# Recurrent attention with an MLP behind it: decay sums over the product of two tokens' w, the diagonal term added on VectorE, and unit 5 transposed by DMA as well

## The chip, the cores and the metric

The kernel runs on one core of one Trainium2 chip. The metric is the device time of one execution in microseconds (us), as the median of several executions. The profile's span, from the first to the last instruction of one profiled execution, is 1.7 to 1.9 us shorter than the device time of the same execution. Stage lengths are read from profiles.

Short names: PE is TensorE (the matrix engine), DVE is VectorE, ACT is ScalarE, POOL is GpSimd.

## The reference

A linear attention with a decay per channel runs over 768 tokens, for 4 sequences and 8 heads of 48 channels. Its output goes through an MLP of 384 by 2048 by 384 with a Gelu.

```python
def _attn_ref(r, k, v, w, u):                       # each (4, 8, 768, 48); u (8, 48)
    state = zeros((B, H, D, D))
    for t in range(S):
        ...                                         # rt, kt, vt, wt: r, k, v, w of token t
        cur = einsum('bhd,bhe->bhde', u[None] * kt, vt)
        y[:, :, t] = einsum('bhd,bhde->bhe', rt, state + cur)
        state = wt[:, :, :, None] * state + einsum('bhd,bhe->bhde', kt, vt)
    return y

def _moe_ref(x, w_in, w_out):                       # x (3072, 384)
    h = x @ w_in                                    # (3072, 2048)
    g = 0.5 * h * (1.0 + tanh(c * (h + 0.044715 * h**3)))
    return g @ w_out
```

The kernel works in *units*: 256 tokens of one sequence, 12 units in all, numbered 0 to 11. Two neighbouring tokens share a partition (the index `t2` tells them apart). The recurrence within a chunk is turned into matrix products: the factors of the decay come from sums of log w over earlier tokens, which are products with a triangular matrix of ones.

## The kernel before

The kernel gives eight PSUM banks to three pools. Two hold MLP tiles (`h`), two hold the down projection (`o`), and four serve everything of the attention (`a`).

```python
ps_h = tile_pool(name="ps_h", bufs=2, space=PSUM)
ps_o = tile_pool(name="ps_o", bufs=2, space=PSUM)
ps_a = tile_pool(name="ps_a", bufs=4, space=PSUM)
```

The decay sums take log w of both tokens of a pair, and add the two on PE by accumulating two matmuls for each sum. The exponentials go back into PSUM, except unit 5's (`sbuf=True`), which are copied to SBUF so that its sums leave their banks early.

```python
def ln(q):
    lw = logws[q % 3]                       # [128, 2, 8, 64]
    ACT.activation(out=lw[:, :, :, 0:D].rearrange("p t h d -> p h t d"),
                   in_=ld["w", q].rearrange("p h (t d) -> p h t d", t=2), func=AF.Ln)

def a1(q, pool=None, tag="a"):
    lw = logws[q % 3]
    x, z = ((pool or ps_a).tile([P, 512], FP, ...) for i in range(2))
    for dst, tri in ((x, strict), (z, incl)):
        for t2 in range(2):
            PE.matmul(dst[:, 0:HD], tri, lw[:, t2, :, 0:D], start=(t2 == 0), stop=(t2 == 1))
    for g in range(G):
        for t2 in range(2):
            PE.matmul(z[:, ds(HD + 2 * g, 2)], lw[:, t2, ds(2 * g, 2), :], ones2, ...)

def exps(q, sbuf=False): ...                # ACT: e1 = exp(-z), fq = exp(x), al = exp(ends)

def prep(q):                                # four DVE products: kk (two, with e1), rq (two, with fq)
    for dst, t2, x, dec in ((kk, 0, kw, e1), (kk, 1, kt[:, :, D:2*D], e1),
                            (rq, 0, rt[:, :, 0:D], fq), (rq, 1, rw, fq)):
        DVE.tensor_tensor(out=dst[...], in0=gjd(x), in1=dec..., op=AL.mult)
    ...                                     # am on POOL
```

The attention of a unit is a generator whose steps are woven between the MLP groups of the unit before it. `...` marks cuts.

```python
PE_T = (6, 6)                               # units below 6 are transposed on PE, later ones by DMA

def attention(q):
    if q < PE_T[...]: a2(q, 0), a2(q, 1); yield     # transposes of kk, rq
    a3(q, 0); yield                         # scores, round 0: 16 matmuls, then two DVE mask products
    a3(q, 1); yield                         # scores, round 1
    a4(q); a4p(q); yield                    # y: scores times v, plus diagonal term; p: state products
    a5(q, 0); yield                         # y += rq times state, first half; then ACT copies y to xs
    a5(q, 1); yield
    a6(q); yield                            # transpose xs for the MLP

def a4(q):
    ...                                     # 32 matmuls y <- scores, v
    for t2 in range(2):                     # the diagonal term, by selection matmuls
        for c2 in range(2):
            PE.matmul(ys[c2][:, :, :], sel...[rows, t2, :], st["vsc", q][rows, t2, :, :], ...)

def a5(q, c2):
    ...
    ACT.activation(out=st["xs", q][:, c2, :], in_=ys[c2]..., func=AF.Copy)

def mm1(q, i):                              # one MLP group: 6 matmuls into one ps_h bank, then its Gelu
    h = ps_h.tile([P, 2, WIN], FP, tag="h")
    ...
    ACT.activation(out=st["g", q][:, ds(2*i, 2), :], in_=h, func=AF.Gelu_apprx_tanh)

for q in range(3, NU):
    att = attention(q + 1) if q + 1 < NU else iter(())
    for i in range(8):
        mm1(q, i)
        if i >= 4:
            mm2(q, 0, (2*i - 8, 2*i - 7))   # two down-projection matmuls
        if i in ((0, 1, 2, 4, 5, 6, 7) if q + 1 < max(PE_T) else (1, 2, 4, 5, 6)):
            next(att, None)
        if q == 3 and i == 4:
            prep(5); ...
        ...                                 # prep_w, prep_a (POOL) at i == 0; a1, prep_b at i == 6
    ...
```

The whole kernel:

## Time and profile before

The time before is 207.69 us, the median of the four runs beside which the changed kernel was timed (207.44 to 208.52). I call *stage q* the stretch from the first MLP matmul of unit q to that of unit q+1. It holds the MLP of unit q and the attention of unit q+1. The stage lengths are read from the timeline of PE:

| stretch | us | what limits it |
|---|---|---|
| up to stage 0 | 22.82 | loads, first unit's attention |
| stages 0, 1, 2, 3 | 19.08, 16.11, 17.88, 16.50 | PE, held in places by DVE |
| stage 4 | 15.40 | PE; still with PE transposes of unit 5 |
| stages 5 to 8 | 14.15, 14.16, 14.15, 14.15 | PE |
| stages 9, 10 | 13.30, 13.30 | PE; no decay sums left to do |
| stage 11 and end | 15.30 | PE, then the last store |

These are two lines of the profile page of the kernel before: busy time and share of the span by engine, and the chain of waits that ended last, by engine.

```profile
PE 184.5 (89%) x2328; PEld 132.9 (64%) x2328; DVE 129.1 (63%) x223; ACT 123.9 (60%) x197; POOL 114.2 (55%) x114
...
PE 75%; DVE 15%; POOL 3%; DMA 2%; ACT 2%; issue 1%; DVEq 0%; ACTq 0%; POOLq 0%
```

Averages over the span hide the stages. This is the busy time by stretch (start and end, length, then the busy time of each engine and its instructions) for stages 3, 7 and 9 of the kernel before (behind the last busy time stand granted clock, DMA share and GB/s):

```profile
75.89:92.39 16.50, 15.20 (x208) 11.32 (x206) 14.06 (x25) 9.82 (x17) 12.21 (x12) 1.00 0.49 111
...
136.10:150.25 14.15, 14.15 (x184) 10.32 (x183) 8.00 (x16) 9.80 (x17) 9.37 (x9) 1.00 0.79 163
...
164.40:177.70 13.30, 13.30 (x171) 9.73 (x170) 5.67 (x11) 8.12 (x12) 0.19 (x1) 1.00 0.39 71
```

In the later stretches PE is busy for the whole stage, so there what leaves PE should leave the time, while DVE (8.00 of 14.15 us) has room. In stage 3 PE is idle for 1.3 us while DVE is busy for 14.06 of 16.50 us. There, work taken from PE may become waiting. The idle time is one wait. In this timeline of PE the columns are start, duration from first start to last end, what, and in brackets the idle time before it and what ended it:

```profile
79.64 0.24 PE L272 MATMUL mt_0_0_1423<-TT_1_1395,TT_0_1384 48*64 48x128 bf16 x2 [1.30 <-DVE TT_1_1395 L255]
```

PE waits for DVE to copy unit 4's transposes out of PSUM before it can start the scores. DVE comes to those copies late because of products ahead of them. One of those, which has both inputs in SBUF, takes 1.84 us (timeline of DVE, before):

```profile
73.37 1.84 DVE L188 TENSOR_TENSOR rw_1332<-r_211,w_201 128x384 f32<-128x384 f32 x1
```

The parts that the change takes from PE have these costs in the PE-bound stages. The duration column of a row reaches past the start of the next row (the two matmuls of `cum_0` last 0.49 us, and the next row starts 0.33 us after their start), so a cost is read from start to start:

```profile
126.96 0.32 PE L301 MATMUL y_0_2376<-vsc_1914,sel 64*128 64x384 bf16 x1
...
127.29 0.20 PE L318 MATMUL p_0_2414<-vb_1724,kk_126 64*128 64x96 bf16 x1
...
130.03 0.49 PE L172 MATMUL cum_0_2469<-logw_122,strict 128*128 128x384 bf16 x2
130.36 0.49 PE L172 MATMUL cum_1_2470<-logw_122,incl 128*128 128x384 bf16 x2
130.68 0.34 PE L176 MATMUL cum_1_2470<-ones_102,logw_122 128*128 128x2 bf16 x8
130.88 0.81 PE L369 MATMUL h_7_2487<-xT_2222,w_in_sb 128*128 128x256 bf16 x6
```

The diagonal term occupies PE from 126.96 to 127.29 (0.33 us) and the decay sums from 130.03 to 130.88 (0.85 us). Last, the MLP groups around the two score rounds of a unit, in the same timeline:

```profile
136.75 0.82 PE L369 MATMUL h_1_2582<-xT_2507,w_in_sb 128*128 128x256 bf16 x6
137.50 0.24 PE L272 MATMUL mt_0_0_2590<-TT_1_2249,TT_0_2246 48*64 48x128 bf16 x2
...
137.85 0.83 PE L369 MATMUL h_2_2611<-xT_2507,w_in_sb 128*128 128x256 bf16 x6
138.61 0.24 PE L272 MATMUL mt_1_0_2619<-TT_1_2249,TT_0_2246 48*64 48x128 bf16 x2
...
138.96 0.83 PE L369 MATMUL h_3_2640<-xT_2507,w_in_sb 128*128 128x256 bf16 x6
139.62 0.82 PE L369 MATMUL h_4_2648<-xT_2507,w_in_sb 128*128 128x256 bf16 x6
140.28 0.49 PE L378 MATMUL o_0_2656<-w_out_sb,g_2564 128*128 128x384 bf16 x2
```

An MLP group alone takes 0.66 us from start to start (138.96 to 139.62). With a score round behind it, it takes 1.10 to 1.11 us (136.75 to 137.85, and 137.85 to 138.96). So the two rounds cost 2.21 − 2 × 0.66 = 0.89 us, and part of that was, by my estimate, the cost of going from one kind of matmul to the other and back.

### The profile page before, as it was taken

To read this page: it belongs to the slowest core of one execution; us is meant where nothing else is said; L and a number is where in the kernel's file an instruction comes from. 1 tells how busy PE (TensorE), PEld (TensorE's weight loads), DVE (VectorE), ACT (ScalarE), POOL (GpSimd) and SP (SyncE) were. 2 spreads that over 40 slices of the span, in tenths; PEclk is the share of its full clock that TensorE was granted. 3 is DMA by queue.
4 is the path that set the end of the run, shared out by engine and by line. 5 is a ranking of instruction groups with operands and counts; after the bars stand their busy time and mean duration, and the time that the engine had idled before them with its cause. 6 is when DMAs were issued, how large, how long until landed. Compare 5 with 4: busy or idle time off the path is not lost.

```text
span 206.3 us, 5543 instructions
## 1 busy us (share of the span) xinstructions
PE 184.5 (89%) x2328; PEld 132.9 (64%) x2328; DVE 129.1 (63%) x223; ACT 123.9 (60%) x197; POOL 114.2 (55%) x114
## 2 busy tenths in 40 slices
PE   0566697998999897999999999999999999999991
PEld 0344484676676565767767767767677677676760
DVE  7846969858667799698665666576373653352111
ACT  3355456765567473594495594785774757457550
POOL 3877737494894988949369468286396300000000
PEclk9999999999999999999999999999999999999998
DMA  6999999999979414906897795985975161200203
GB/s 160 273 392 344 327 340 302 238 264 262 225 189 227 102 41 106 239 22 99 189 220 103 164 246 92 231 180 105 229 92 89 43 102 41 67 12 19 61 0 76
DMA packets 70024, 33.58 MB, mean 163 GB/s; under 512 B 63984, under 2 KB 69232, under 8 KB 70000
## 3 DMA queue, kind: packets, MB, share of 16 engines
q1 hardware_dynamic: 70000, 33.24, 70.1%
q8 instruction: 18, 0.29, 0.6%
q14 instruction: 6, 0.05, 0.1%
HBM read 25.36 MB, written 4.72 MB: 146 GB/s over the span
## 4 chain that ended last, share of the span: by engine, by line
PE 75%; DVE 15%; POOL 3%; DMA 2%; ACT 2%; issue 1%; DVEq 0%; ACTq 0%; POOLq 0%
DMA w_89<-in_w_dram 2%; PE o_1_3620 L378 1%; PE o_0_1489 L378 1%; PE o_0_2921 L378 1%; PE o_0_2373 L378 1%; PE o_0_2088 L378 1%; PE o_0_3574 L378 1%; PE o_0_2656 L378 1%; PE o_0_3396 L378 1%; PE o_1_3512 L378 1%; PE o_1_3292 L378 1%; PE o_1_3072 L378 1%; PE o_1_2808 L378 1%; PE o_1_2537 L378 1%; PE o_1_2252 L378 1%; PE o_1_1967 L378 1%
## 5 line engine op out<-in xcount | busy, mean ns | idle before, releaser
L369 PEld LDWEIGHTS <-w_in_sb 128*128 128x128 bf16 x576 | 54.1, 99 | 13.2 <-issue 3.0
L157 ACT ACT_TABLE_LOAD x13 | 16.7, 1283 | 0.9 <-PEq L585 0.7
L159 ACT ACT_TABLE_LOAD x12 | 15.4, 1283 | 0.2
L172 PEld LDWEIGHTS <-strict 128*128 128x128 bf16 x24 | 1.8, 100 | 6.6 <-issue 4.9
L172 PE MATMUL cum_0_219<-logw_122,strict 128*128 128x384 bf16 x2 | 0.8, 502 | 5.5 <-ACT logw_122 L163 5.5
L386 DVE COPY ob_3616<-o_0_3574 128x384 f32<-128x384 f32 x1 | 0.6, 558 | 7.7 <-PE o_0_3574 L378 7.7
L378 PEld LDWEIGHTS <-g_440 128*128 128x128 bf16 x32 | 2.8, 97 | 3.0 <-issue 1.4
L378 PE MATMUL o_0_558<-w_out_sb,g_440 128*128 128x384 bf16 x16 | 3.6, 327 | 1.1 <-DVE w_out_sb L86 1.1
L378 PEld LDWEIGHTS <-g_3533 128*128 128x128 bf16 x32 | 3.1, 98 | 1.6
L378 PEld LDWEIGHTS <-g_2829 128*128 128x128 bf16 x32 | 3.1, 98 | 1.5
L378 PEld LDWEIGHTS <-g_1689 128*128 128x128 bf16 x32 | 3.1, 98 | 1.5
L378 PEld LDWEIGHTS <-g_1375 128*128 128x128 bf16 x32 | 3.1, 98 | 1.5
L378 PEld LDWEIGHTS <-g_2281 128*128 128x128 bf16 x32 | 3.1, 98 | 1.5
L378 PEld LDWEIGHTS <-g_2564 128*128 128x128 bf16 x32 | 3.1, 98 | 1.5
L378 PEld LDWEIGHTS <-g_3313 128*128 128x128 bf16 x32 | 3.1, 98 | 1.5
L378 PEld LDWEIGHTS <-g_1996 128*128 128x128 bf16 x32 | 3.1, 98 | 1.5
L378 PEld LDWEIGHTS <-g_3093 128*128 128x128 bf16 x32 | 3.1, 98 | 1.5
L207 POOL TENSOR_TENSOR vsc_530<-vb_434,dg_529 128x768 bf16<-128x768 bf16 x1 | 1.7, 1662 | 4.3 <-DVE dg_529 L206 4.3
L378 PEld LDWEIGHTS <-g_745 128*128 128x128 bf16 x32 | 2.8, 98 | 1.7
L172 PEld LDWEIGHTS <-incl 128*128 128x128 bf16 x24 | 2.5, 106 | 2.0 <-issue 0.7
L378 PEld LDWEIGHTS <-g_1046 128*128 128x128 bf16 x32 | 2.7, 97 | 1.6
L242 POOL TENSOR_TENSOR am_708<-blk,al_680 128x384 f32<-128x384 bf16 x2 | 1.9, 987 | 2.9 <-ACT al_680 L222 2.9
(895 smaller groups left out, 645.2 us busy)
## 6 DMA issues: line engine op xcount, KB each, us to landing
wi_157<-in_moe_w_in_dram SPq DMA_DIRECT2D x1, 512.0 KB, 5.0
wi_159<-in_moe_w_in_dram SPq DMA_DIRECT2D x1, 512.0 KB, 6.1
wi_161<-in_moe_w_in_dram SPq DMA_DIRECT2D x1, 512.0 KB, 6.9
wi_163<-in_moe_w_in_dram SPq DMA_DIRECT2D x1, 512.0 KB, 7.7
wi_165<-in_moe_w_in_dram SPq DMA_DIRECT2D x1, 512.0 KB, 8.5
wi_167<-in_moe_w_in_dram SPq DMA_DIRECT2D x1, 512.0 KB, 9.4
w_89<-in_w_dram SPq DMA_DIRECT2D x1, 384.0 KB, 3.7
k_91<-in_k_dram SPq DMA_DIRECT2D x1, 384.0 KB, 4.7
```

Of the source, the lines that this page charges most:

```text
L157: ACT.preload_act_table_set(EXP_SET)
L159: ACT.preload_act_table(AF.Gelu_apprx_tanh)
L172: PE.matmul(dst[:, 0:HD], tri, lw[:, t2, :, 0:D], start=(t2 == 0), stop=(t2 == 1))
L207: POOL.tensor_tensor(out=vsc, in0=vb, in1=dg.rearrange("p h t -> p t h")[:, :, :, None].broadcast_to([P, 2, H, D]), op=AL.mult)
L242: POOL.tensor_tensor(out=am[:, c2], in0=blk.rearrange("p g j d -> p g (j d)"), in1=al[:, :, c2][:, :, None].broadcast_to([P, G, 2 * D]), o ...
L369: PE.matmul(h[:, f, :], w_in_sb[:, cb, ts(ft, P)], xT[:, :, cb, :], start=(f + cb == 0), stop=(cb == NCB - 1), skip_group_check=True)
L378: PE.matmul(st["o", q, c2], g[:, ft, ts(c2, P)], w_out_sb[:, ft, :], start=(ft == 0), stop=(ft == NFT - 1))
L386: DVE.tensor_copy(out=ob[:, c2, :], in_=st.pop(("o", q, c2)))
```

## The change

Four ideas are in it.

1. *Decay sums halved.* log(w0) + log(w1) = log(w0 w1). The product of the two tokens' w is formed first (`ww`, on POOL, for unit 0 on DVE). One Ln of half the elements follows, and the sums need one matmul where they needed two.
2. *Diagonal term on DVE.* From unit 6, the four selection matmuls go, and so do ACT's two copies of y out of PSUM. Four DVE additions bring y out of PSUM and add the diagonal term on the way. They are half-height (64 partitions each), as the two tokens of a pair lie in different halves.
3. *Unit 5 also by DMA transpose.* That takes its 16 transposes off PE and the two copies off DVE. For this its exponentials stay in PSUM (its first sum in an `a` bank, its second in an `o` bank), and its four products move up, ahead of unit 4's state operations.
4. *Score rounds merged* from unit 6: both rounds run behind MLP group 1, instead of behind groups 1 and 2.

The diff, cut to its core:

```diff
-    logws = [pfix.tile([P, 2, H, 64], BF, ...) for i in range(3)]
+    logws = [pfix.tile([P, H, 64], BF, ...) for i in range(3)]
-    PE_T = (6, 6)
+    PE_T = (5, 5)
+    DVE_DIAG = 6
+    MERGE = 6
     def ln(q):
-        ... (both tokens' w)
+        ACT.activation(out=logws[q % 3][:, :, 0:D], in_=st.pop(("ww", q)), func=AF.Ln)
+    def ww(q, eng=POOL):
+        wt = ld["w", q]
+        t = pw2.tile([P, H, D], FP, tag="ww", name=f"ww{q}")
+        eng.tensor_tensor(out=t, in0=wt[:, :, 0:D], in1=wt[:, :, D:2 * D], op=AL.mult)
+        st["ww", q] = t
     def a1(q, ...):
-            for t2 in range(2):
-                PE.matmul(dst[:, 0:HD], tri, lw[:, t2, :, 0:D], start=(t2 == 0), stop=(t2 == 1))
+            PE.matmul(dst[:, 0:HD], tri, lw[:, :, 0:D], start=True, stop=True)
...
     def a4(q):
-        for t2 in range(2):
+        for t2 in range(2 if q < DVE_DIAG else 0):
...
     def a5(q, c2):
+        if q >= DVE_DIAG:
+            for t2 in range(2):
+                rows = ds(64 * t2, 64)
+                DVE.tensor_tensor(out=st["xs", q][rows, c2, :]..., in0=ys[c2][rows, :, :],
+                                  in1=st["vsc", q][ds(64 * c2, 64), t2, :, :], op=AL.add)
+            return
         ACT.activation(out=st["xs", q][:, c2, :], in_=ys[c2]..., func=AF.Copy)
...
     def attention(q):
         a3(q, 0)
-        yield
+        if q < MERGE:
+            yield
         a3(q, 1)
...
         if q == 2:
-            a1(5)
-            exps(5, True)
+            a1(5, (0, 1))
+            exps(5)
...
-            if q == 3 and i == 4:
+            if q == 3 and i == 2:
                 prep(5)
+            if i == 0 and q + 4 < NU:
+                ww(q + 4)
```

More of the change, by code (lines that the diff above doesn't have):

```diff
@@ L125 @@
     make_identity(nc, ident)
-    logws = [pfix.tile([P, 2, H, 64], BF, name=f"logw{i}") for i in range(3)]
+    logws = [pfix.tile([P, H, 64], BF, name=f"logw{i}") for i in range(3)]
     kk_ps = [pfix.tile([P, G, 2, 2, 64], BF, name=f"kk{i}") for i in range(3)]
@@ L161, in ln, with a1 @@
     def ln(q):
-        lw = logws[q % 3]
-        ACT.activation(
-            out=lw[:, :, :, 0:D].rearrange("p t h d -> p h t d"),
-            in_=ld["w", q].rearrange("p h (t d) -> p h t d", t=2), func=AF.Ln)
-    def a1(q, pool=None, tag="a"):
-        lw = logws[q % 3]
-        x, z = ((pool or ps_a).tile([P, 512], FP, tag=tag, name=f"cum{q}_{i}") for i in range(2))
+        ACT.activation(out=logws[q % 3][:, :, 0:D], in_=st.pop(("ww", q)), func=AF.Ln)
[4 more added lines that the diff above has]
+        st["ww", q] = t
+    def a1(q, pools=(0, 0)):
+        lw = logws[q % 3]
+        x, z = ((ps_a, ps_o)[p].tile([P, 512], FP, tag="ao"[p], name=f"cum{q}_{i}")
+                for i, p in enumerate(pools))
         for dst, tri in ((x, strict), (z, incl)):
-            for t2 in range(2):
-                PE.matmul(dst[:, 0:HD], tri, lw[:, t2, :, 0:D], start=(t2 == 0),
-                          stop=(t2 == 1))
+            PE.matmul(dst[:, 0:HD], tri, lw[:, :, 0:D], start=True, stop=True)
         for g in range(G):
-            for t2 in range(2):
-                PE.matmul(z[:, ds(HD + 2 * g, 2)], lw[:, t2, ds(2 * g, 2), :], ones2,
-                          start=False, stop=(t2 == 1), skip_group_check=True)
+            PE.matmul(z[:, ds(HD + 2 * g, 2)], lw[:, ds(2 * g, 2), :], ones2,
+                      start=False, stop=True, skip_group_check=True)
         st["cum", q] = (x, z)
@@ L211, in prep_b, with exps @@
         st["vsc", q] = vsc
-    def exps(q, sbuf=False):
+    def exps(q):
         x, z = (t[:, 0:HD] for t in st["cum", q])
@@ L216, in exps @@
         fq, e1 = x, z
-        if sbuf:
-            fq, e1 = (pw2.tile([P, HD], BF, tag=t, name=f"{t}{q}", bufs=1) for t in ("fq", "e1"))
         al = pw2.tile([P, G, 2], FP, tag="al", name=f"al{q}", bufs=3)
@@ L297, in a4 @@
                               skip_group_check=True)
-        for t2 in range(2):
+        for t2 in range(2 if q < DVE_DIAG else 0):
             for c2 in range(2):
@@ L344, in a5 @@
             st["xs", q] = xs
+        if q >= DVE_DIAG:
+            for t2 in range(2):
+                rows = ds(64 * t2, 64)
+                DVE.tensor_tensor(
+                    out=st["xs", q][rows, c2, :].rearrange("p (h d) -> p h d", h=H),
+                    in0=ys[c2][rows, :, :], in1=st["vsc", q][ds(64 * c2, 64), t2, :, :],
+                    op=AL.add)
+            return
         ACT.activation(out=st["xs", q][:, c2, :], in_=ys[c2].rearrange("p h d -> p (h d)"),
@@ L438 @@
     table("exp")
+    ww(0, DVE)
     ln(0)
@@ L444 @@
     prep_a(0)
+    ww(1)
     ln(1)
@@ L451 @@
     next(att)
-    a1(1, ps_o, "o")
+    a1(1, (1, 1))
     exps(1)
@@ L479 @@
         if q > 0:
+            ww(q + 3)
+            if q == 2:
+                ww(6)
             prep_a(2 * q + 1)
@@ L485 @@
         if q == 0:
+            ww(2)
             ln(2)
@@ L511 @@
         mm2(q, 0, range(14, 16))
+        if q == 0:
+            ww(3)
         ln(q + 3)
         if q == 2:
-            a1(5)
-            exps(5, True)
+            a1(5, (0, 1))
+            exps(5)
             ln(6)
@@ L536 @@
                 mm2(q, 0, (2 * i - 8, 2 * i - 7))
-            if i in ((0, 1, 2, 4, 5, 6, 7) if q + 1 < max(PE_T) else (1, 2, 4, 5, 6)):
+            if i in ((0, 1, 2, 4, 5, 6, 7) if q + 1 < max(PE_T) else (1, 2, 4, 5, 6) if q + 1 < MERGE else (1, 4, 5, 6)):
                 next(att, None)
-            if q == 3 and i == 4:
+            if q == 3 and i == 2:
                 prep(5)
```

## The prediction

It was written before the changed kernel had run. One passage is cut from it, where the cut is marked: the reason for counting 0.55 to 0.6 us for a half-height addition. What stays there is my estimate. It counts the 0.55 us that the trace shows a full-height product to last, with a little added, and not the 0.47 us from start to start.

> **What bounds it now.** From unit 4 on, TensorE. The page's first part has PE busy 184.5 of 206.3 us; the chain of waits is 75% PE, 15% VectorE. In the order of time, the MLPs start at 92.39, 107.95, 122.10, 136.25, 150.40, 164.55, 177.85, 191.15: stages of 14.15 us (13.30 without decay sums) in which PE is never idle (busy time by stretch: 14.10 of 14.10). In the first 80 us VectorE (transpose copies, diagonal reduction, mask products) holds PE at 29.7-35.3, 46.8-51.5, 63.0-71.3 and up to 79.6, where PE waits 1.30 us for a transpose copy.
>
> **Removed from PE** (start to start in the trace):
> - Decay sums: 0.85 us per unit (130.03 to 130.88); half goes: 0.42, 12 units.
> - Diagonal matmuls: 126.96 to 127.29, 0.32 us, units 6-11.
> - Unit 5's transposes: stage 4 lasts 15.55 against 14.15 us; those 1.4 us go.
> - Merged score rounds: two rounds cost 0.89 us beyond the MLP matmuls around them (122.60 to 124.81); about half is entering and leaving. Merging saves an estimated 0.22 us, units 6-11.
>
> **Added.** GpSimd: a 128x384 product per unit, about 1.0 us (as its others), in idle time late on, but in a full stretch at 65-91 us. VectorE: one product before the first Ln; in units 6-11 four half-height adds. 384-element PSUM products take 0.55 us, 0.47 start to start. [...] I take 0.55-0.6 each, 2.3 us per unit (estimate; no instruction of this trace shows it). ScalarE loses two 0.49 us copies and half of each 0.85 us Ln.
>
> **On the critical path.**
> - Start: the product before Ln delays the first sums by about 0.7 us; GpSimd's chain (mask copies, am, rk to 14.1 us) hides it: 0 +- 0.4.
> - Stages 0, 1: -0.42 each.
> - Stage 2: two units' sums, 0.85, lost in the 1.30 us wait, as the VectorE chain to 79.6 is unchanged.
> - Stage 3: unit 5's first sum stays in one of four PSUM banks until its four VectorE products, now after the mask products. The built program puts unit 4's second state product there: PE stalls about 0.9 us, against 0.42 saved. Net +0.5.
> - Stage 4: -1.8.
> - Stages 5, 6: -0.97 each, 0.4 given back: the adds come behind four state operations; transposes and sums wait for VectorE by 0.1-0.3.
> - Stages 7, 8: -0.97 each; 9, 10: -0.54 each.
>
> Sum: -0.85 +0.5 -1.8 -1.1 -1.95 -1.1 = -6.3 us.
>
> **Prediction: 201.4 us, 199.7 to 203.6** in 8 of 10. Faster by over 2%: 0.88; within 2%: 0.11; slower: 0.01.
>
> **What would show it.** Stages of 13.7 us (4), 13.2 (7, 8), 12.8 (9, 10). PE idle about 0.9 us before unit 4's second state product, ended by VectorE. PE's wait before unit 4's score matmuls over 1.3 us. Small waits before the last transposes in stages 5, 6. VectorE about +10 us, GpSimd +11, ScalarE -10, PE -8.
>
> **What would make it wrong.** Half-height adds costing far more than 0.6 us: stages 5-10 would wait for them. GpSimd's two extra products at 65-70 us delaying unit 4's or 6's operands, or slowing VectorE's two-SBUF-input products (0.54 us alone, 1.10 to 2.15 beside GpSimd): up to +2 us. No stall in stage 3: -0.9. Merging saving nothing: +1.3.

## More of the kernel before

Executions quoted here: the mean granted TensorE clock of the profiled ones is 0.99 to 1.00. It was halved for 3.4 us in the middle of one of them, e3_fq_sbuf, as is told there.

## The result

The changed kernel takes **202.77 us** (median of 4 runs, 202.50 to 203.24), against 207.69 us before. The ratio is **0.976**, with a 95% interval of 0.973 to 0.979. Here and below a ratio is the mean time of one kernel's fast runs over that of the other's fast runs of the same rounds, so it is not quite the ratio of the medians. The results of both kernels are correct. The prediction of 201.4 us was 1.4 us too low. The measured time lies inside its range of 199.7 to 203.6 us.

The lines of the profile page after the change that answer to those of before, with one group from its list of the costliest (count, busy time, mean ns of one):

```profile
PE 176.2 (88%) x2216; PEld 127.3 (63%) x2216; DVE 142.2 (71%) x246; ACT 114.8 (57%) x185; POOL 124.8 (62%) x125
...
PE 71%; DVE 21%; issue 3%; POOL 3%; ACT 1%; DVEq 0%; ACTq 0%
...
L349 DVE TENSOR_TENSOR xs<-y,vsc 64x384 bf16<-64x384 f32 x24 | 13.3, 554 | 0.7
```

PE lost 8.3 us of work, but the span shrank only by 5.4 us. The stages show where it went. The middle columns are the lengths in the two profiled executions.

| stretch | before | after | difference | predicted |
|---|---|---|---|---|
| up to stage 0 | 22.82 | 22.86 | +0.04 | 0 |
| stage 0 | 19.08 | 18.93 | −0.15 | −0.42 |
| stage 1 | 16.11 | 15.69 | −0.42 | −0.42 |
| stage 2 | 17.88 | 17.02 | −0.86 | 0 (with stage 3: +0.5) |
| stage 3 | 16.50 | 17.34 | +0.84 | +0.5 |
| stage 4 | 15.40 | 13.73 | −1.67 | −1.8 |
| stages 5, 6 | 28.31 | 27.21 | −1.10 | −1.1 |
| stages 7, 8 | 28.30 | 26.72 | −1.58 | −1.95 |
| stages 9, 10 | 26.60 | 25.87 | −0.73 | −1.1 |
| stage 11 and end | 15.30 | 15.53 | +0.23 | 0 |
| sum | 206.3 | 200.9 | −5.4 | −6.3 |

**Stages 2 and 3.** Timeline of PE, after:

```profile
78.61 0.42 PE L273 MATMUL mt<-TT,TT 48*64 48x128 bf16 x16 [1.30 <-DVE TT L256]
...
82.63 0.20 PE L319 MATMUL p<-vb,kk 64*128 64x96 bf16 x1
83.46 0.50 PE L319 MATMUL p<-vb,kk 64*128 64x96 bf16 x15 [0.62 <-DVE rq L238]
83.89 0.83 PE L378 MATMUL h<-xT,w_in_sb 128*128 128x256 bf16 x6
```

The wait of 1.30 us before unit 4's scores is still there, so PE still follows DVE there. The moment itself moved from 79.64 to 78.61 us. About half of this was gained before stage 2 began, and the other half because DVE's chain in stage 2 got 0.5 us shorter. Its product of r and w takes 1.35 us where it took 1.84. In POOL's timeline it lay beside one instruction of 1.81 us before (72.99 to 74.80), and lies beside instructions of 1.31 us each after (timeline of DVE, after, with the last of unit 5's products behind it):

```profile
72.83 1.35 DVE L191 TENSOR_TENSOR rw<-r,w 128x384 f32<-128x384 f32 x1
...
82.86 0.55 DVE L238 TENSOR_TENSOR rq<-rw,cum 128x384 bf16<-128x384 f32 x1
```

The second wait is new: PE issues one state product of unit 4 at 82.63 and stands until DVE's last product of unit 5, which starts at 82.86, has ended. In the built program the second state product of unit 4 gets the PSUM bank of unit 5's first decay sum, and that product is the sum's last reader. From the scores to the next stage the kernel takes 13.23 us (78.61 to 91.84), against 12.75 before (79.64 to 92.39). That is +0.48 us, with 0.42 us of decay sums already saved in it, so the stall with its surroundings costs 0.9 us. From start to start the stall itself is 0.83 us (82.63 to 83.46).

**Stages 5 to 10.** Timeline of PE, after, at the merged rounds of stage 7. The `mt` row has both rounds, and the second `h` row has the three MLP groups behind them:

```profile
132.78 1.47 PE L378 MATMUL h<-xT,w_in_sb 128*128 128x256 bf16 x12
134.18 0.64 PE L273 MATMUL mt<-TT,TT 48*64 48x128 bf16 x32
134.76 2.33 PE L378 MATMUL h<-xT,w_in_sb 128*128 128x256 bf16 x18
136.92 0.49 PE L387 MATMUL o<-w_out_sb,g 128*128 128x384 bf16 x2
```

With 0.655 us for an MLP group alone, the two rounds together now take 134.76 − 132.78 − 2 × 0.655 = 0.67 us, where they took 0.89. That is the saving that was predicted, 0.22 us. But the three groups behind them take 136.92 − 134.76 = 2.16 us instead of 3 × 0.655 = 1.97. ACT's timeline of the same stretch shows what could cause it:

```profile
133.63 1.25 ACT L380 ACTIVATE g<-h 128x512 bf16<-128x512 f32 x2 [0.78 <-PE h L378]
135.62 1.25 ACT L380 ACTIVATE g<-h 128x512 bf16<-128x512 f32 x2 [0.73 <-PE h L378]
```

Only two PSUM banks hold MLP groups. The groups 2, 3 and 4 now come without a pause, and group 4 needs the bank that the Gelu of group 2 (135.62 to about 136.2) has to read first. The chain of waits starts group 4 at 136.27 after "issue" time at 136.24, just behind that Gelu.

**Half-height additions.** Timeline of DVE, after, stage 5 (the attention of unit 6):

```profile
113.42 2.27 DVE L349 TENSOR_TENSOR xs<-y,vsc 64x384 bf16<-64x384 f32 x4
115.72 0.95 DVE L209 TENSOR_REDUCE dg<-rk 128x16 f32<-128x768 f32 x1
```

Four take 2.30 us from start to start, 0.57 us each. A full-height product of DVE from PSUM starts 0.46 us after the one before it (81.47, 81.93, 82.39, 82.86 for the four of unit 5) although each lasts 0.55 us. The half-height additions last 0.54 to 0.56 us, and each starts 0.01 to 0.03 us after the one ahead of it has ended. Why they do not overlap as the products do is not shown: no run here varied the halves alone.

### The profile page after: what moved, and what is told of

Read it like the earlier page. It is cut to its first block, busy times and chain, and to the rows that moved or that the text cites. A ratio compares the mean times of both kernels' runs of the same rounds, so it can differ in the third digit from the quotient of the medians.

```text
span 200.9 us, 5332 instructions
## 1 busy us (share of the span) xinstructions
PE 176.2 (88%) x2216; PEld 127.3 (63%) x2216; DVE 142.2 (71%) x246; ACT 114.8 (57%) x185; POOL 124.8 (62%) x125
## 4 chain that ended last, share of the span: by engine, by line
PE 71%; DVE 21%; issue 3%; POOL 3%; ACT 1%; DVEq 0%; ACTq 0%
PE h L378 30%; PE o L387 27%; DVE mtsb L279 6%; DVE TT L256 3%; PE y L296 2%; DVE dg L209 2%; PE p L319 2%; PE mt L273 2%; PE xTp L363 2%; PE y L341 1%; PE cum L177 1%; PE y L302 1%; DVE rq L238 1%; POOL rk L200 1%; DVE w_out_sb L86 1%
## 5 line engine op out<-in xcount | busy, mean ns | idle before, releaser
L380 ACT ACTIVATE g<-h 128x512 bf16<-128x512 f32 x96 | 57.3, 597 | 57.1 <-PE h L378 55.5
L378 PE MATMUL h<-xT,w_in_sb 128*128 128x256 bf16 x576 | 75.7, 277 | 1.7 <-DVE xT L364 1.3
L387 PE MATMUL o<-w_out_sb,g 128*128 128x384 bf16 x384 | 72.4, 326 | 1.6 <-DVE w_out_sb L86 1.4
L387 PEld LDWEIGHTS <-g 128*128 128x128 bf16 x384 | 36.2, 98 | 20.6 <-issue 2.0
L279 DVE TENSOR_TENSOR mtsb<-mt,mask 128x512 bf16<-128x512 f32 x48 | 29.9, 683 | 7.2 <-PE mt L273 7.2
L210 POOL TENSOR_TENSOR vsc<-vb,dg 128x768 bf16<-128x768 bf16 x12 | 18.0, 1503 | 20.1 <-DVE dg L209 20.1
L395 DVE COPY ob<-o 128x384 f32<-128x384 f32 x24 | 13.3, 552 | 15.1 <-PE o L387 13.8
L200 POOL TENSOR_TENSOR rk<-rk,u_bc 128x768 f32<-128x768 f32 x12 | 22.1, 1844 | 0.9
L198 POOL TENSOR_TENSOR rk<-k,r 128x768 f32<-128x768 f32 x12 | 22.0, 1836 | 0.4 <-DMA r<-in_r_dram 0.4
L243 POOL TENSOR_TENSOR am<-blk,al 128x384 f32<-128x384 bf16 x24 | 20.0, 856 | 3.5 <-ACT al L223 2.8
```

Of the source, the lines that this page charges most:

```text
L198: POOL.tensor_tensor(out=rk, in0=kt.rearrange("p h (t d) -> p h t d", t=2), in1=rt.rearrange("p h (t d) -> p h t d", t=2), op=AL.mult)
L200: POOL.tensor_tensor(out=rk, in0=rk, in1=u_bc[:, :, None, :].broadcast_to([P, H, 2, D]), op=AL.mult)
L210: POOL.tensor_tensor(out=vsc, in0=vb, in1=dg.rearrange("p h t -> p t h")[:, :, :, None].broadcast_to([P, 2, H, D]), op=AL.mult)
L243: POOL.tensor_tensor(out=am[:, c2], in0=blk.rearrange("p g j d -> p g (j d)"), in1=al[:, :, c2][:, :, None].broadcast_to([P, G, 2 * D]), o ...
L279: DVE.tensor_tensor(out=sb[:, j], in0=mts[j], in1=mask.rearrange("p a b t -> p a (b t)")[:, None, :, :].broadcast_to([P, 2, 2, P]), op=AL. ...
L378: PE.matmul(h[:, f, :], w_in_sb[:, cb, ts(ft, P)], xT[:, :, cb, :], start=(f + cb == 0), stop=(cb == NCB - 1), skip_group_check=True)
```

## The experiments

Eleven kernels were run, each five rounds against the kernel before. All gave correct results. The first four ran on one chip, and the others in groups on other chips; each has its own runs of the kernel before beside it. The kernel before gave medians of 207.77, 207.75, 207.42 and 207.85 us in the four groups of runs (the first four, the next four, the next two, the last).

| label | edit | us | ratio (95%) | stages 3, 4, 5, 6, 7, 8, 9, 10 in us |
|---|---|---|---|---|
| (changed kernel) | | 202.77 | 0.976 (0.973–0.979) | 17.34 13.73 13.60 13.61 13.36 13.36 12.93 12.94 |
| e1_no_merge | rounds not merged | 203.31 | 0.977 (0.974–0.980) | 17.33 13.73 13.65 13.65 13.40 13.40 12.97 12.98 |
| e2_space | merged, down projection sooner | 200.85 | 0.966 (0.963–0.969) | 17.32 13.73 13.41 13.42 13.17 13.17 12.74 12.75 |
| e1b_no_merge_space | both edits | 202.97 | 0.976 (0.972–0.979) | 17.32 13.73 13.64 13.65 13.40 13.40 12.97 12.98 |
| e3_fq_sbuf | unit 5's exp(x) in SBUF | 206.08 | 0.991 (0.987–0.994) | 20.84 13.73 13.61 13.60 13.36 13.36 12.94 12.93 |
| e4_pe_diag | diagonal on PE again | 203.69 | 0.981 (0.979–0.984) | 17.34 13.73 13.69 13.68 13.69 13.68 13.26 13.26 |
| e5_rq_first | unit 5's rq products first | 201.62 | 0.970 (0.968–0.973) | 16.51 13.73 13.60 13.61 13.36 13.36 12.93 12.94 |
| e6_pe_t5 | unit 5 on PE again | 204.20 | 0.982 (0.980–0.985) | 17.33 14.97 13.61 13.61 13.35 13.37 12.93 12.93 |
| e7_decay_alone | before, with halved sums only | 206.24 | 0.993 (0.990–0.995) | 16.81 16.31 13.73 13.72 13.73 13.73 13.30 13.30 |
| e8_both | e2 and e5, last stage reordered | 200.88 | 0.968 (0.966–0.971) | 16.50 13.73 13.41 13.42 13.17 13.17 12.74 12.75 |
| e9_all | e8 and repairs in stages 0 to 2 | 199.98 | 0.964 (0.961–0.967) | 16.51 13.73 13.41 13.42 13.17 13.17 12.74 12.75 |
| e10_last | e9, last stage repaired | 200.03 | 0.963 (0.959–0.966) | 16.49 13.73 13.41 13.42 13.17 13.17 12.74 12.74 |

The stages repeat from kernel to kernel to 0.02 us, while the times scatter by about half a microsecond. Stage 0 is the reason, or at least one: its length in the profiled execution ran from 18.8 to 19.7 us in the changed kernel and the kernels that have its stage 0, and was 17.6 and 18.6 us in e9_all and e10_last, which share one edit there. It lies in the first 36 MLP matmuls: without them stage 0 is 12.70 or 12.71 us long in the changed kernel and all of e1 to e8. These are the lines of the changed kernel, of e8_both and of e9_all, in three timelines of PE:

```profile
22.86 6.22 PE L378 MATMUL h<-xT,w_in_sb 128*128 128x256 bf16 x36 [1.28 <-DVE xT L364]
```

```profile
22.87 6.96 PE L379 MATMUL h<-xT,w_in_sb 128*128 128x256 bf16 x36 [1.29 <-DVE xT L365]
```

```profile
22.35 5.84 PE L379 MATMUL h<-xT,w_in_sb 128*128 128x256 bf16 x36 [0.77 <-DVE xT L365]
```

The same 36 matmuls took 6.22, 6.96 and 5.84 us. In the kernel before, the second and third groups of six each took 1.28 us from start to start, and later groups 0.65. In the traces half pace comes first and full pace later (in the changed kernel the matmuls of a group start 0.213 us apart up to 26.65 us, and 0.109 us apart from 26.87 us), and the clock record in the trace files, which the views do not print, opens with a full clock at 26.86, 28.78 and 25.57 us in these three, at most 0.1 us before the first matmul at full pace (the views count the time before the record as full clock). In the thirteen profiled executions here it came 3.2 to 5.9 us after the first MLP matmul, at 25.57 to 28.78 us, and the first 36 MLP matmuls took between 5.84 and 6.96 us. So the moment varies by 3.2 us; what sets it is not shown. I therefore read stages.

### Is the merging's saving eaten by the wait for a Gelu?

The theory: merging does save 0.22 us per unit, but makes three MLP groups follow one another, and the third waits for a PSUM bank until a Gelu has read it. The rival: merging saves nothing by itself, or the missing time is DVE's. Three kernels tell these apart: one without merging, one with merging in which two down-projection matmuls stand ahead of group 4 (so that PE has other work while the Gelu runs), and a control that moves those matmuls without merging.

```diff
-    MERGE = 6
+    MERGE = 12
```

> The changed kernel with the two score rounds of units 6 to 11 apart again. Theory A (merging takes away the work between MLP groups that hid the Gelu: groups 2, 3, 4 now run back to back and group 4 waits about 0.19 us for ScalarE to empty its PSUM bank, so that merging is worth only about 0.03 us a stage): stages 7 and 8 become 13.41 us instead of 13.36, stages 9 and 10 12.98 instead of 12.93, whole time +0.1 to +0.3 us, near 203.0. Theory B (as predicted: merging saves 0.22 us a stage and the missing 0.18 us is lost elsewhere): stages 7 and 8 13.58, whole time +1.3 us, near 204.1.

```diff
-            if i >= 4:
+            if q + 1 >= MERGE and i == 3:
+                mm2(q, 0, (0, 1))
+            if i >= 4 and not (q + 1 >= MERGE and i == 4):
                 mm2(q, 0, (2 * i - 8, 2 * i - 7))
```

> The changed kernel with the first two down-projection matmuls of stages 5 to 11 ahead of MLP group 4 instead of behind it; same work. Theory A: the 0.17 us wait of group 4 for the Gelu of group 2 goes, stages 5 to 10 each get 0.15 to 0.19 us shorter (7 and 8: 13.18; 9 and 10: 12.75), whole time -1.0 us or a little more, near 201.7. Theory B: stages stay at 13.36 and 12.93, whole time within 0.2 us of the changed kernel.

The control has `MERGE = 12` and the second edit with the condition `q >= 5` in place of `q + 1 >= MERGE`.

> Control: score rounds apart again and the two down-projection matmuls ahead of group 4. Theory A: without merging no group waits for the Gelu, so moving the two matmuls gains nothing: same as the kernel with the rounds apart (within 0.2 us, near 203.0), and 1.2 to 1.4 us slower than the one that merges and moves. If moving the two matmuls helps for another reason, this one gains about 1 us as well.

Measured: without merging the stages 7 to 10 are 0.04 us longer than with it (13.40 against 13.36, 12.97 against 12.93). So merging, as the change has it, is worth 0.04 us a stage; the times (203.31 and 202.77 us) are too close to tell the two kernels apart. With the two matmuls moved, the merged stages 5 to 10 get 0.19 to 0.20 us shorter each (13.36 to 13.17), and in the control these stages gain nothing (13.40). This is the timeline of PE of e2_space, at the same place as above:

```profile
133.60 0.64 PE L273 MATMUL mt<-TT,TT 48*64 48x128 bf16 x32
134.18 1.48 PE L378 MATMUL h<-xT,w_in_sb 128*128 128x256 bf16 x12
135.50 0.49 PE L387 MATMUL o<-w_out_sb,g 128*128 128x384 bf16 x2
135.82 0.82 PE L378 MATMUL h<-xT,w_in_sb 128*128 128x256 bf16 x6
136.57 0.57 PE L296 MATMUL y<-vb,mtsb 64*128 64x48 bf16 x32
```

The two groups behind the rounds take 1.32 us (134.18 to 135.50), that is twice 0.66: no wait is left. The theory holds. The saving of 0.22 to 0.23 us is there once the wait is gone (13.40 without merging, 13.17 with it), and 0.19 us of it had become a wait for a Gelu. In time e2_space is also clearly faster than the control: 0.966 against 0.976, of the same rounds.

### Is the stall in stage 3 the bank of unit 5's first sum?

The theory: unit 4's second state product waits for the bank in which unit 5's first sum is still read. Two kernels attack it. One keeps exp(x) of unit 5 in SBUF, as the kernel before did, so that the bank is free early. The other lets the readers of that bank go first among the four products.

```diff
-    def exps(q):
+    def exps(q, sbuf=False):
...
+        if sbuf:
+            fq = pw2.tile([P, HD], BF, tag="fq", name=f"fq{q}", bufs=1)
...
-            exps(5)
+            exps(5, True)
```

> The changed kernel with unit 5's exponential of the first sum written to SBUF, so that its PSUM bank is free at once. Theory C (PE's 0.62 us idle before unit 4's second state product is the wait for that bank): the idle goes, stage 3 falls from 17.34 to about 16.7 us, whole time -0.5 to -0.7 us, near 202.1. Rival D (VectorE's row of four products ahead of the state operations sets stage 3, the bank only shows it): idle before the second product goes, but PE waits later for the state sum, stage 3 stays within 0.2 us of 17.34.

```diff
-        for dst, t2, x, dec in ((kk, 0, kw, e1), ...):
+        four = ((kk, 0, kw, e1), (kk, 1, kt[:, :, D:2 * D], e1),
+                (rq, 0, rt[:, :, 0:D], fq), (rq, 1, rw, fq))
+        for dst, t2, x, dec in (four[2:] + four[:2] if q == 5 else four):
```

> The changed kernel with unit 5's two products that read the first sum done before the two that read the second: same work, the PSUM bank comes free 0.93 us earlier. Theory C (PE's 0.62 us idle before unit 4's second state product is the wait for that bank, and nothing else waits behind it): the idle goes, stage 3 falls from 17.3 to about 16.7 us, whole time -0.6 us, near 202.3. Rival D (the VectorE row of products ahead of the state operations sets stage 3): stage 3 stays within 0.2 us of 17.3.

The second one settles it. In e5_rq_first the 16 state products run without a wait, and stage 3 goes from 17.34 to 16.51 us. Timeline of PE, e5_rq_first:

```profile
83.02 0.50 PE L320 MATMUL p<-vb,kk 64*128 64x96 bf16 x16
```

The 0.83 us gained is the stall from start to start. DVE does the same four products ahead of the state operations in both kernels, so it is their order, and not their time, that set the stall.

The first one removed the wait too, but missed otherwise: stage 3 rose to 20.84 us. The timeline of DVE of e3_fq_sbuf shows the same two products that took 0.55 us from PSUM, and a wait of PE's for the state behind them is in its timeline of PE:

```profile
82.90 2.19 DVE L240 TENSOR_TENSOR rq<-r,fq 128x384 bf16<-128x384 f32 x1
85.01 2.16 DVE L240 TENSOR_TENSOR rq<-rw,fq 128x384 bf16<-128x384 f32 x1
```

```profile
88.36 0.33 PE L343 MATMUL y<-S,TT 128*128 128x96 bf16 x4 [2.56 <-DVE S L332]
```

This wait is not the whole of the loss. Behind it the granted clock of PE was halved for 3.41 us. This is the busy time of that stretch (the third number from the end is the granted clock):

```profile
89.75:93.16 3.41, 3.41 (x17) 2.01 (x15) 1.31 (x2) 3.30 (x7) 1.91 (x2) 0.50 0.25 38
```

PE was busy in all of it, so by an estimate from these figures half of it, 1.7 of the 3.5 us by which stage 3 is longer than in the changed kernel, is the clock, and the rest is the slower products less the wait that was removed. What halved the clock is not shown. Five of the six executions have a mean clock of 0.990 to 0.992; the one with 0.998 was the fastest, 204.77 us, and still slower than the changed kernel.

Now the products themselves.

With both inputs in SBUF they take 2.19 and 2.16 us, four times as long. POOL is at work throughout. The first of the two products starts at 82.90 us, just behind the start of a POOL product that runs from 82.83 to 84.67, and ends 0.4 us after it; the second meets the next POOL product, of 2.00 us, in the same way. It is no accident of this run: in the traces of the kernels before and after, of e3_fq_sbuf and of e7_decay_alone, every such product that starts after 22 us, while a POOL instruction is running, ends 0.41 or 0.42 us after that instruction. In these traces such a product thus takes what is still to come of the POOL instruction, and 0.41 or 0.42 us more. With POOL idle it takes 0.54 to 0.55 us (87.81, 88.28 and 88.75 us in the kernel before). So the copy to SBUF, which looks like a harmless way to free a bank, is not one here.

### What are the other parts of the change worth?

The diagonal back on PE for all units, and unit 5 back on PE transposes:

```diff
-    DVE_DIAG = 6
+    DVE_DIAG = 12
```

> The changed kernel with the diagonal term of units 6 to 11 on TensorE again (four matmuls, ScalarE copies out). If the four VectorE adds cost PE about 0.25 us in stages 5 and 6 (waits before the sums and the transposes) and nothing later: stages 5 and 6 13.67 instead of 13.60, stages 7 and 8 13.68 instead of 13.36, stages 9 and 10 13.25 instead of 12.93; whole time +1.4 us, near 204.2. Rival: the adds cost nothing and the 0.25 us in stages 5 and 6 has another cause: stages 5 and 6 at 13.92, whole time +1.9 us.

```diff
-    PE_T = (5, 5)
+    PE_T = (6, 6)
```

> The changed kernel with unit 5 transposed by TensorE again. As predicted for the DMA transpose (0.9 us of matmuls and the wait around them, with 0.42 of the 1.67 us due to the halved sums): stage 4 about 15.0 instead of 13.73 us, all other stages within 0.1, whole time +1.25 us, near 204.1. Rival: the wait around the transposes would have gone anyway, since PE now meets VectorE elsewhere: stage 4 14.6, +0.9.

With the diagonal on PE, stages 7 to 10 are longer by 0.32 or 0.33 us (13.69 against 13.36, 13.26 against 12.93). That is the 0.33 us that it occupies PE. Stages 5 and 6 are longer by only 0.08 us (13.69 and 13.68 against 13.60 and 13.61): there the DVE additions come with small waits of PE, 0.25 us a stage, which give most of it back. Read from start to start, stage 5 of the changed kernel loses 0.11 us against stage 7 at the decay sums and 0.12 to 0.13 us at the last transposes, where the prediction had put these waits. Half-height additions are therefore not what the missing time of stages 7 to 10 came from.

With unit 5 on PE, stage 4 goes from 13.73 to 14.97 us. The 1.24 us, with the 0.42 us of halved sums, is the 1.67 us that the change gained in that stage.

### What do the halved sums give alone?

This is the kernel before with the `ww`, `ln`, `a1` and `logws` parts of the change and nothing else.

> The kernel before with the halved decay sums alone (product of the two tokens' w, on GpSimd). If each halved sum is worth 0.42 us where PE bounds the stage: stages 4 to 8 each 0.42 us shorter than before (14.98, 13.73 four times), stages 9 and 10 unchanged at 13.30, stage 1 0.42 shorter, stage 0 about 0.2 shorter (a weight cast beside GpSimd takes longer), stages 2 and 3 together 0.4 to 1.3 shorter; whole time -3.1 to -4.0 us, near 204.2. Rival: GpSimd's added 1 us a unit delays other things and takes a part back in stages 4 to 8: less than 0.3 us each, whole time -2 us.

Stages 5 to 8 got 0.42 us shorter each (14.15 to 13.73), as the 0.85 us for sums in the trace would have it. But the kernel gained only 0.7% in all, because stage 4 rose from 15.40 to 16.31 us, a miss. Timeline of DVE, then of PE, of e7_decay_alone:

```profile
86.30 1.17 DVE L237 TENSOR_TENSOR kk<-k,e 128x384 bf16<-128x384 f32 x1
87.40 1.18 DVE L237 TENSOR_TENSOR rq<-r,fq 128x384 bf16<-128x384 f32 x1
88.50 1.18 DVE L237 TENSOR_TENSOR rq<-rw,fq 128x384 bf16<-128x384 f32 x1
```

```profile
95.04 0.42 PE L272 MATMUL mt<-TT,TT 48*64 48x128 bf16 x16 [1.62 <-DVE TT L255]
```

In the kernel before, these three products took 0.54 and twice 0.55 us. POOL was idle then, and here it is still busy until 89.3 us with work that the added `ww` products pushed back. DVE comes out of them no earlier than before (at 89.6 us against 89.2), although PE is 1.3 us ahead by then, and PE waits 1.62 us for a transpose copy in place of 0.28. What lets the halved sums pay in stage 4 is therefore the move of unit 5's exponentials to PSUM with the earlier place of its products; these two were not tested apart. The DMA transposes are not needed for it: e6_pe_t5 keeps the transposes on PE, and its stage 4 is 14.97 us, 0.43 us shorter than before.

### A version that beats both

e8_both joins the two repairs (e2_space and e5_rq_first), and in the last stage starts the down projection after the third MLP group. e9_all adds two repairs near the start. Unit 3's `ww` goes to DVE, behind the cast that it held up, and in stages 1 and 2 four down-projection matmuls of the unit before fill the MLP groups.

```diff
+            if q == NU - 1:
+                if i >= 2:
+                    mm2(q, 0, (2 * i - 4, 2 * i - 3))
...
-        mm2(q, 0, range(8, 12))
+        mm2(q, 0, range(8 if q < NU - 1 else 12, 12))
```

> The changed kernel with both repairs (two down-projection matmuls ahead of MLP group 4 in stages 5 to 10; unit 5's products that free the PSUM bank first), and in the last stage the down-projection spread from group 2 on. If the two waits are independent and all on TensorE's path the gains add: stage 3 16.5, stages 5 to 10 as in the run with the two matmuls moved (13.41, 13.41, 13.17, 13.17, 12.75, 12.75), last stage 0.2 to 0.4 us shorter; whole time near 199.9. Rival: what one repair gives another wait takes back: 200.5 or more.

```diff
+            if q > 0 and i in (1, 3):
+                mm2(q - 1, 1, (11 + i, 12 + i))
+                if i == 3:
+                    store(q - 1, 1)
...
-            ww(3)
+            ww(3, DVE)
...
-        mm2(q, 1, range(16))
-        store(q, 1)
+        mm2(q, 1, range(16 if q == 2 else 12))
+        if q == 2:
+            store(q, 1)
```

> The same with the spacing of MLP groups also in stages 1 and 2 (four down-projection matmuls of the unit before kept back and put behind groups 1 and 3) and with unit 3's product of w on VectorE, away from the weight cast that it slowed. If the Gelu waits (0.19 us each, two a stage) are the same in these stages: stages 1 and 2 each 0.3 to 0.4 us shorter in sum of start to start, and the 0.23 us wait for the cast in stage 0 gone; whole time near 199.1. Rival: VectorE sets these stages (its transpose copies and mask products), so that PE's earlier groups only wait longer there: within 0.3 us of the run without.

In e8_both the gains of both repairs stand side by side in the stages (16.50 and 13.17 us). Its last stage did not get shorter, a miss. Its time, 200.88 us, is no better than that of e2_space, 200.85 us, although its stage 3 is 0.8 us shorter; a time of 200.5 us or more is what the rival expected. The two profiles show where the 0.82 us went. The first 36 matmuls of stage 0, in which no edit lies, took 6.96 us against 6.12; the clock rose at 28.78 us in e8_both, the latest of all the profiled executions. And the last stage's MLP took 11.06 us against 10.85: the edit of e2_space reaches stage 11 too and had shortened it, and e8_both puts another edit in its place. Whether the other executions went the same way is not shown.

The expectation for e9_all held in part. Four down-projection matmuls (0.65 us) pass from stage 0 to stage 1 and from stage 1 to stage 2. With these counted, and without the first 36 matmuls, stage 0 gained 0.28 us, stage 1 0.16 us and stage 2 0.38 us against the changed kernel, where 0.23 and twice 0.3 to 0.4 had been expected. Its time is 199.98 us, not 199.1.

e10_last is e9_all with the last stage's down projection started one group later:

```diff
-                if i >= 2:
-                    mm2(q, 0, (2 * i - 4, 2 * i - 3))
+                if i >= 3:
+                    mm2(q, 0, (2 * i - 6, 2 * i - 5))
...
-        mm2(q, 0, range(8 if q < NU - 1 else 12, 12))
+        mm2(q, 0, range(8 if q < NU - 1 else 10, 12))
```

> The kernel with all repairs (e9_all), but in the last stage the down projection starts after the fourth MLP group instead of the third, so that two more of its matmuls (six in place of four... counted in pairs of groups: those of groups 5 to 7) stay behind the last MLP group. Why: in e8_both and e9_all the last stage did not get shorter, although the waits for PSUM banks among its MLP groups went from about 0.43 to 0.24 us. Theory: the gain was handed back at the end, where the last four of the 22 down-projection matmuls after the last MLP group (3.95 us) come too soon after it and wait about 0.2 us for its Gelu, which the 26 of the changed kernel (4.39 us, 0.163 us each) did not. It expects the last MLP stage's TensorE time, first MLP matmul to end of the last down-projection matmul, to be about 10.85 us here, against 11.04 in the changed kernel and 11.06 in e8_both. Rival: the last stage is limited by something else (the loading of weights, the pace of ScalarE over all eight groups), and it stays at 11.04 to 11.06. Other stages as in e9_all: 13.73, 13.41, 13.42, 13.17, 13.17, 12.74, 12.75. Total 199.8 us, 198.8 to 201, ratio 0.960 to 0.968.

These are the last rows in PE's timeline of the changed kernel, of e8_both and of e10_last:

```profile
192.02 4.39 PE L387 MATMUL o<-w_out_sb,g 128*128 128x384 bf16 x26
```

```profile
191.27 3.95 PE L388 MATMUL o<-w_out_sb,g 128*128 128x384 bf16 x22
```

```profile
189.81 4.06 PE L388 MATMUL o<-w_out_sb,g 128*128 128x384 bf16 x24
```

From the first MLP matmul of the last stage to the end of the last row takes 11.04 us in the changed kernel (from 185.37), 11.06 in e8_both (from 184.16) and 10.86 in e10_last (from 183.01). The expectation was 10.85. In e8_both the last row has four matmuls fewer than in the changed kernel, but is only 0.44 us shorter and not 4 × 0.163 = 0.65: it holds a wait of 0.2 us. The last Gelu of that kernel ends at 192.07 us, 0.8 us into the row, and the last two of the unit's first 16 down-projection matmuls need it: four stand ahead of them in the row, and six in e10_last. In e10_last two fewer shorten it by 0.33 us, as they should. So the first attempt had moved one wait for a Gelu to another place, and the second removed it. It only restores what e2_space had, 10.85 us. The time after the last matmul is 4.90 us in e9_all and e10_last and 4.48 us in the changed kernel, so from stage 11 to the end e10_last takes 15.75 us and gains nothing there; the cause of that tail was not studied.

e9_all (199.98 us, ratio 0.964) and e10_last (200.03 us, ratio 0.963) are the fastest kernels. Both beat the kernel before and the changed kernel. Between them, and against e2_space (0.966), the intervals overlap, and the times do not tell which is best.

## Why the prediction was right or wrong

The time fell inside the range, and most steps came out as written. The estimate promised 0.9 us more than the profiled spans show, −6.3 against −5.4 us; the medians differ by 4.9 us. That it came so close is in part luck: 0.5 us gained in stage 2, for a reason that it did not have, hides part of what it missed elsewhere. The terms are these:

- **The step that failed: "Merging saves an estimated 0.22 us, units 6-11".** Where the stage depended on nothing else (7 to 10), the prediction gave 0.97 and 0.54 us and got 0.79 and 0.37, short by about 0.18 us a stage, 0.7 us in all. The runs show that the rounds did get 0.22 us cheaper, and that 0.19 us of this came back as a wait for the Gelu of the group two before, because three MLP groups now follow one another on two PSUM banks. Unmerging cost 0.04 us, and filling the wait gave 0.19. Among its risks the prediction had "Merging saving nothing: +1.3", and that is nearly what happened. ACT's Gelu of 0.60 us and the two banks were both in the trace and in the code, and the place behind the rounds should have been checked for them.
- **Stages 5 and 6 were right only in sum.** The prediction gave 0.97 us a stage less 0.4 for waits. Measured are waits of 0.25 us, less than predicted, and a merging that is worth 0.04 us. The two errors cancel: −1.10 measured, −1.1 predicted.
- **Stage 3, "Net +0.5", held as a mechanism and as a size.** From the scores to the end of the stage the change costs 0.48 us. Reordering the four products removes 0.83 us, which shows that the late readers of unit 5's first sum, and so its bank, were the cause.
- **Stage 2, "0.85, lost in the 1.30 us wait, as the VectorE chain to 79.6 is unchanged", was wrong in its reason.** PE's wait stayed at 1.30 us, so its own saving was indeed lost there. But DVE's chain did change: one product beside POOL took 1.35 us instead of 1.84, and the scores came 0.5 us earlier for it. The prediction had named this contention only as a danger. In the two traces that product meets a POOL instruction of 1.81 us before and of 1.31 us after, in line with what e3_fq_sbuf shows of such meetings. No run varied this alone, so it is read and not tested. That the sum of stages 2 and 3 came out at −0.02 us and not +0.5 is this 0.5 us.
- **Stage 4, "−1.8", held:** −1.67, of which e6_pe_t5 gives 1.24 us back.
- **Stage 0 fell short** (−0.15 against −0.42). Without its first 36 matmuls, which took 6.45 us before and 6.22 us after, it did not get shorter at all: 12.63 us before, 12.71 us after. The 0.42 us of sums are saved, but 0.51 us comes back just behind them, 0.10 us before the last transposes and 0.41 us at them. 0.23 us of this is a wait of PE for a weight cast of DVE, which takes 0.83 us and not 0.55, beside the added `ww` product of POOL. In e9_all, which moved that product to DVE, the wait is gone and 0.28 us is won back. The rest was not studied.
- **The end,** +0.23 us against 0, lies behind the last matmul: the last stage's MLP takes 11.04 us in both kernels, and what follows 4.24 us before and 4.48 us after. It was not studied.
- **Half-height additions, "0.55-0.6 each",** came out at 0.57 us. Their 2.3 us per unit fit into DVE's idle time from stage 7 on, and the diagonal's whole 0.33 us was gained there.
- **Busy time:** PE −8.3 us (−8 predicted), ACT −9.1 (−10), POOL +10.6 (+11), DVE +13.1 (+10). DVE's term was underestimated, without consequence in the later stages.

What stays open: whether the moment at which the clock rises in stage 0, taken here as most of the reason why the profiled e8_both was no faster than e2_space, is that for their times as well; and why the time behind the last matmul differs between kernels.

## What to carry to other kernels

When you put two pieces of work together to save the switching between them, look at what now stands back to back: here three MLP groups met two PSUM banks, and 0.19 of the 0.22 us saved became a wait that two matmuls of other work filled in e2_space. Before you move a tile from PSUM to SBUF to free its bank, ask who else reads SBUF at that moment: a VectorE product with two SBUF inputs took two to four times as long beside GpSimd (1.17 to 1.18 us in e7_decay_alone and 2.16 to 2.19 us in e3_fq_sbuf, against 0.54 to 0.55 us with GpSimd idle). And when a stage holds a wait, a saving ahead of that wait is worth what the engine that ends the wait allows, so cost that engine's chain, not the one that waits.
